# Relu-squared attention and an FFN on one core: when the casting transfers start, when beta is made, and where the first FFN1 matmuls stand

## The chip, the cores and the metric

The kernel runs on one core of a Trainium2 chip. A core has four compute engines that run their own instruction streams: TensorE (PE, matmuls), VectorE (DVE), ScalarE (ACT) and GpSimd (POOL). SyncE (SP) issues transfers; ACT and POOL can issue transfers as well. All transfers of the core are carried by its 16 DMA engines. Transfers issued by POOL may change the type on the way (here float32 in memory to bfloat16 on the core); those issued by SP and ACT copy as they are. The metric is the device time of the whole program in microseconds (us); lower is better.

## The reference

Inputs are q, k, v of shape (8, 12, 448, 64), two weight matrices and a vector alpha, all float32.

```python
scores = scale * np.matmul(q, k.transpose(0, 1, 3, 2))     # scale = 1/8
attn = np.maximum(scores, 0.0) ** 2 / S                    # S = 448
x = np.matmul(attn, v)                                     # (8, 12, 448, 64)
x = x.transpose(0, 2, 1, 3).reshape(3584, 768)
h = x @ w_in                                               # 768 -> 2048
g = np.maximum(h, 0.0) + alpha * np.minimum(h, 0.0)        # alpha: one value for each of 2048
out = g @ w_out                                            # 2048 -> 768, float32
```

There is no softmax: a score is clipped at zero and squared. Each (batch, head) pair is independent in the attention; the FFN mixes the 12 heads of a batch.

## The kernel before, in words

**Quads.** Four heads of one batch make a quad; a batch has three, so there are 24 quads, numbered 0 to 23. The 448 positions of a head are 64 times 7. A score block `j` (0 to 6) of a quad holds 64 key positions of each of the four heads against all 448 queries: four matmuls of 64x64 weights and 448 columns, into two halves of PSUM (`score_mm`, L158).

**One quad's work.** `load` (float32, from SP) or `load_bf16` (casting, from POOL, L102) brings k, q and v. `transpose` (L133, L108) turns k and q on PE for quads 0 to 5 and copies the result out of PSUM into `kT` and `qT`; later quads are turned by transfers. `scores` runs one block and clips it at zero on ACT, on DVE, or half on each ("both"); `squares2` squares two blocks at once on DVE (L202). `attnv` (L233) multiplies the seven squared blocks with v, and its result is scaled into `xT` (L242 to L248).

**The FFN.** `ffn1(b, ff, kms)` (L262) makes 128 of the 2048 columns of one batch in six steps `km` of 128 rows, two steps for each quad of the batch: km 0 and 1 need quad 0, km 2 and 3 quad 1, km 4 and 5 quad 2. ACT then makes `neg` (L269) and DVE combines it with `beta = 1 - alpha` (L270). `ffn2` (L278) does the second matrix for two batches together.

**Order.** The schedule is written by hand: each engine runs its instructions in the order in which the program emits them, and waits at an instruction until what it needs is there. Buffers come from pools that rotate: the tile asked for next takes the oldest buffer, and its first writer waits for the last reader of what was in it. Pools that matter here: `mm_ps` (four PSUM banks, tags "mm"), `sc_ps` (two), and `early_pool` (two buffers for each of k and q in bfloat16, so that quad 2's k takes the buffer of quad 0's).

**The start.** `warm(18)` (L367) runs 18 matmuls on zeros. SP loads quad 0's raw q, then its raw k in two parts (blocks 0 to 2, then 3 to 6), then alpha (L373 to L378). POOL makes two identity matrices and issues the casting loads of quad 1's k and q and of v for quads 0 and 1 (L381 to L384). DVE and ACT cast quad 0's q and k (L386 to L392), PE turns them. The loop at L398 then goes through the blocks of quads 0 to 2, with the transposes of the next quad at blocks 3 and 4, and `attnv` of the quad before at block 2. After quad 0's blocks, alpha (16 by 128) is turned on PE into a column for each of 128 rows (L422), DVE makes beta (L423), and POOL's next loads are emitted: quad 2, w_in in three pieces, quad 3. In the last quad of the loop, blocks 4, 5 and 6 are each followed by the first four km of one `ffn1` of batch 0 (L419).

**After the start.** Batch 0's remaining FFN1 and the blocks of quads 3, 4 and 5 are interleaved by a list (L458 to L466), in which `turn(n)` transposes quad n. The rest of the program, from L477, spreads score blocks of later batches between FFN matmuls.

Of the kernel before, what the change touches and what calls it, by code (L numbers as in the profile page):

```python
# [10 lines left out]
F32 = mybir.dt.float32  # L11
BF16 = mybir.dt.bfloat16
ACTF = mybir.ActivationFunctionType
ALU = mybir.AluOpType
# [6 lines left out]
NJ = 7  # L21
# [3 lines left out]
def kernel(  # L25
# [10 lines left out]
    nc = tc.nc  # L36
    B, H, S, D = q.shape
# [5 lines left out]
    KF = d_ff // 128  # L43
# [4 lines left out]
    def pool(name, bufs, **kw):  # L48
        return ctx.enter_context(tc.tile_pool(name=name, bufs=bufs, **kw))
# [6 lines left out]
    early_pool = pool("early", 2)  # L56
# [10 lines left out]
    mm_ps = pool("mmps", 4, **PSUM)  # L67
# [3 lines left out]
    alpha_sb = singles.tile([KF, 128], F32)  # L71
    beta_sb = singles.tile([128, KF], F32)
    ident_f = singles.tile([KF, KF], F32)
# [5 lines left out]
    raw, cast, qT, kT, vb = {}, {}, {}, {}, {}  # L79
    src = {"q": q, "k": k, "v": v}  # L80

    def flat(n, w):
        b, g = quads[n]
        return src[w][b, 4 * g:4 * g + 4].rearrange("(s hf) (pp j) d -> (hf pp) s (j d)", hf=2, j=NJ)
# [10 lines left out]
    def load_bf16(n, names="kqv"):  # L95

        for w in names:
            if w == "v":
                t = vb[n] = v_pool.tile([128, 2, NJ, D], BF16, tag="v", name="vb")
            else:  # L100
                t = cast[(n, w)] = early_pool.tile([128, 2, NJ, D], BF16, tag=w, name=f"{w}e")
            nc.gpsimd.dma_start(out=t.rearrange("p s j d -> p s (j d)"), in_=flat(n, w))  # L102

    def copy(eng, o, i):
        if eng is nc.scalar:
            nc.scalar.copy(o, i)
        else:
            eng.tensor_copy(o, i)  # L108
# [12 lines left out]
    def transpose(n, w, js=range(NJ), eng=None):  # L121
        store = qT if w == "q" else kT
        if n not in store:
            store[n] = qkT_pool.tile([128, NJ, 2, PP], BF16, tag=w, name=f"{w}T")
        t, dst = cast[(n, w)], store[n]
        if n >= n_pe:
            nc.sync.dma_start_transpose(out=dst.rearrange("p j h c -> p j (h c)"),
                                        in_=t.rearrange("p j s d -> p (j s d)"))
            return
        ps = mm_ps.tile([128, NJ, 2 * PP], BF16, tag="mm", name="tps")  # L130
        for j in js:
            for s in range(2):
                nc.tensor.transpose(ps[64 * s:64 * s + 64, j], t[:, s, j], ident)  # L133
        lo, hi = js[0], js[-1] + 1
        copy(eng or nc.vector, dst[:, lo:hi].rearrange("p j h c -> p j (h c)"), ps[:, lo:hi])
# [4 lines left out]
    def load_w_in(lo, hi):  # L140
        for hf in range(2):
            for e in range(2):
                nc.gpsimd.dma_start(out=w_in_sb[64 * hf:64 * hf + 64, :, e, lo:hi],
                                    in_=w_in_v[hf, e, :, :, lo:hi])
# [37 lines left out]
    def scores(n, j, relu="act", space=sc_ps, pair=False):  # L182

        ps, half = score_tile(space)
        score_mm(n, j, half)
        rl = relu_tile(pair)
        if relu in ("both", "act2"):
            relu_half(rl, half, 0, nc.scalar)
            relu_half(rl, half, 1, nc.vector if relu == "both" else nc.scalar)
        elif relu == "dve":  # L190
            nc.vector.tensor_scalar(rl, ps[:, :, :S], 0.0, None, ALU.max)
        else:
            nc.scalar.activation(rl, ps[:, :, :S], ACTF.Relu)  # L193
        todo.append((n, j, rl))

    def squares2(keep=0):

        while len(todo) >= 2 + keep:
            two = [todo.pop(0) for _ in range(2)]
            t = pairs.pop(0)  # L200
            a = at2_pool.tile([128, 2, 2, S], BF16, tag="at2", name="atp")
            nc.vector.tensor_tensor(a, t, t, ALU.mult)  # L202
            for i, (n, j, _) in enumerate(two):
                att[(n, j)] = a[:, i]
# [50 lines left out]
    def ffn1(b, ff, kms=range(KM)):  # L255
        if b % 2 == 0 and ff == 0 and kms[0] == 0:
            gT[b // 2] = g_pool.tile([128, KF, 2 * S], BF16, tag="g", name="gT")
        if kms[0] == 0:
            hps[ff] = mm_ps.tile([128, S], F32, tag="mm", name="hps")
        ps = hps[ff]  # L260
        for km in kms:
            nc.tensor.matmul(ps, w_in_sb[:, km // 2, km % 2, bass.ts(ff, 128)],  # L262
                             xT[b][:, km // 2, km % 2, :],
                             start=(km == 0), stop=(km == KM - 1))
        if kms[-1] != KM - 1:
            return

        neg = neg_pool.tile([128, S], F32, tag="neg", name="neg")
        nc.scalar.activation(neg, ps, ACTF.Relu, scale=-1.0)  # L269
        nc.vector.scalar_tensor_tensor(gT[b // 2][:, ff, (b % 2) * S:(b % 2) * S + S],  # L270
                                       neg, beta_sb[:, ff:ff + 1], ps, ALU.mult, ALU.add)
# [91 lines left out]
    def warm(count):  # L363

        ps = sc_ps.tile([128, 2, 512], F32, tag="sc", name="warm")
        for _ in range(count):
            nc.tensor.matmul(ps[:, 0, :256], warm_w, warm_x, start=True, stop=True)  # L367

    for w in "qk":
        raw[(0, w)] = raw_pool.tile([128, 2, NJ, D], F32, tag=w, name=f"{w}raw")  # L370
        cast[(0, w)] = early_pool.tile([128, 2, NJ, D], BF16, tag=w, name=f"{w}e")
    first, rest = range(0, 3), range(3, NJ)
    nc.sync.dma_start(out=raw[(0, "q")].rearrange("p s j d -> p s (j d)"), in_=flat(0, "q"))  # L373
    for js in (first, rest):
        lo, hi = js[0], js[-1] + 1
        nc.sync.dma_start(out=raw[(0, "k")][:, :, lo:hi].rearrange("p s j d -> p s (j d)"),
                          in_=flat(0, "k")[:, :, lo * D:hi * D])
    nc.sync.dma_start(out=alpha_sb, in_=moe_alpha.rearrange("(kf p) -> kf p", p=128))  # L378
    make_identity(nc, ident)
    make_identity(nc, ident_f)  # L380
    load_bf16(1, "k")  # L381
    load_bf16(1, "q")
    load_bf16(0, "v")
    load_bf16(1, "v")  # L384
    warm(18)
    nc.vector.tensor_copy(cast[(0, "q")][:, 0], raw[(0, "q")][:, 0])  # L386
    nc.scalar.copy(cast[(0, "q")][:, 1], raw[(0, "q")][:, 1])
    transpose(0, "q")
# [5 lines left out]
    scores(0, 1, pair=True)  # L394
    scores(0, 2, "both", mm_ps, pair=True)
    transpose(0, "k", rest)
    squares2(keep=1)
    for n in range(NG):  # L398
        last = n == NG - 1
        for j in range(NJ):  # L400
            if n == 0 and j < 3:
                continue
            if last and j == 6:
                scores(n, j)
                squares2()
            elif j == 5 and not last or j == 2:
                scores(n, j, "both", mm_ps, pair=True)
            else:
                scores(n, j, "dve" if last and j == 4 else "act", pair=True)
            if not (last and j == 6):  # L410
                squares2(keep=1)
            if j == 2 and n > 0:
                attnv(n - 1, space=mm_ps)
            if j == 3 and not last:
                transpose(n + 1, "k")
            if j == 4 and not last:
                transpose(n + 1, "q")
            if last and j >= 4:
                ffn1(0, j - 4, range(0, 4))  # L419
        if n == 0:  # L420
            ps = mm_ps.tile([128, KF], F32, tag="mm", name="aps")
            nc.tensor.transpose(ps, alpha_sb, ident_f)  # L422
            nc.vector.tensor_scalar(beta_sb, ps, -1.0, 1.0, ALU.mult, ALU.add)  # L423
            load_bf16(2)
            load_w_in(0, 512)
            load_w_in(512, 1024)
            load_w_in(1024, 2048)
            load_bf16(3)
# [4 lines left out]
    attnv(2, range(0, 4), apart=True)  # L433
    attnv(2, range(4, NJ))
    ffn1(0, 3, range(0, 4))
    def turn(n):
        return lambda: (transpose(n, "k", eng=nc.scalar), transpose(n, "q"))

# [16 lines left out]
    for ff in range(4):  # L455
        ffn1(0, ff, range(4, KM))
    f = [fn for _, fn in steps(0, "in")]
    play([f[4], f[5], f[6], turn(3), f[7], f[8], g("30", "31", "32"), f[9], f[10], f[11], f[12],  # L458
          g("33", "34", "35"), f[13], f[14], f[15]])
    load_bf16(5)  # L460
    load(6, after=w_out_sb[:, 0, 384:385])
    load(7)
    o = [lambda c=c, hf=hf, h=h: ffn2(0, c, hf, h) for hf in range(2) for c in range(3) for h in range(2)]
    play([g("36"), turn(4), o[0], o[1], g("40", "41", "3a"), o[2], o[3], g("42", "43", "44"), o[4], o[5],
          g("45", "46"), o[6], turn(5), o[7], g("50", "51", "4a"), feed(6, "k", "q"), o[8], o[9],
          g("52", "53", "54"), feed(6, "v"), o[10], g("55", "56"), feed(7, "k", "q"), o[11]])  # L466

# [64 lines left out]
```

## Time and profile before

| what | value |
|---|---|
| median of 6 runs | 398.9 us (397.05 to 400.43) |
| the profiled execution | 398.75 us, of which its span 397.0 |
| PE busy | 385.8 us |
| DVE, ACT, POOL busy | 261.0, 220.4, 72.5 us |
| casting queue (q0) | 9.96 MB written on the core, 15.9% of the 16 DMA engines' time over the span |
| plain loads and stores from SP (q1) | 44.78 MB, 43.9% |
| raw q of quad 0, issued / its casts begin | 0.74 / 4.08 us |
| second part of raw k, its cast begins | 8.17 us |
| alpha, issue to landing | 6.1 us, issued at 2.26 |

The span runs from the first to the last instruction of the profiled execution, and times in the text are counted from its start. The page cuts the span into 40 equal slices and gives each engine's busy share of a slice in tenths. "The chain that ended last" is followed back from the last instruction, at each step to what released it. A row of a timeline gives start, length, engine, line, operation, written tile <- read tiles, and in brackets how long the engine had stood idle before it and what ended that. For transfers, q0 are the casting ones that POOL issues, q1 those of SP, q10 those of ACT.

### The profile page before, as it was taken

How to read it: one execution, taken by the hardware profiler on the slowest of the kernel's cores; microseconds unless marked ns; L12 is line 12 of the kernel's file. 1: busy time of each engine (PE TensorE's matmuls, PEld its weight loads, DVE VectorE, ACT ScalarE, POOL GpSimd, SP SyncE). 2: the span in 40 equal slices, each digit the busy share in tenths (PEclk: the TensorE clock that was granted, in tenths of full speed). 3: DMA queues.
4: the chain of work that ended last, by engine and by line, in shares of the span. 5: the costliest groups of instructions: out<-in, count | busy, mean ns of one | idle time of the engine just before them, and what ended most of it. 6: DMA issues, size and time to landing. Idle time of an engine off the chain costs nothing.

```text
span 397.0 us, 7955 instructions
## 1 busy us (share of the span) xinstructions
PE 385.8 (97%) x3213; PEld 201.7 (51%) x3213; DVE 261.0 (66%) x406; ACT 220.4 (56%) x345; POOL 72.5 (18%) x87
## 2 busy tenths in 40 slices
PE   7898999999999999999999999999999999999996
PEld 4444555445555455544555445554555545555564
DVE  3976955677675877577665897768575676636421
ACT  5875856675555674466553765556455475624200
POOL 4764000022032430032020550032002300000000
PEclk9899999999999999999999999999999999999999
DMA  8999998593579923492097951295048820120033
GB/s 173 145 207 206 203 216 275 129 302 43 150 139 218 291 84 88 110 294 47 2 216 216 263 163 30 68 265 175 2 132 179 223 46 2 41 74 7 0 81 79
DMA packets 64756, 55.44 MB, mean 140 GB/s; under 512 B 35776, under 2 KB 60496, under 8 KB 64720
## 3 DMA queue, kind: packets, MB, share of 16 engines
q1 hardware_dynamic: 53504, 44.78, 43.9%
q0 software_dynamic: 10976, 9.96, 15.9%
q8 instruction: 25, 0.41, 0.4%
q10 hardware_dynamic: 240, 0.20, 0.2%
q14 instruction: 11, 0.09, 0.1%
HBM read 45.62 MB, written 11.01 MB: 143 GB/s over the span
## 4 chain that ended last, share of the span: by engine, by line
PE 86%; DVE 5%; DMA 4%; ACT 2%; issue 1%; SPq 0%; ACTq 0%; DVEq 0%
PE ops L278 36%; PE hps L262 32%; PE av L233 7%; PE sc L158 5%; PE sch L158 4%; DMA qe<-in_q_dram 3%; DVE at L213 2%; DMA kraw<-in_k_dram 2%; PE ops L301 1%; PE tps L133 1%; DVE atp L202 1%; ACT rl L193 1%; DVE rlp L167 1%; ACT rl L165 1%; DVE gT L270 0%
## 5 line engine op out<-in xcount | busy, mean ns | idle before, releaser
L262 PE MATMUL hps<-xT,w_in_sb 128*128 128x448 bf16 x768 | 151.1, 353 | 1.6 <-DVE gT L270 1.0
L278 PE MATMUL ops<-w_out_sb,gT 128*128 128x384 bf16 x864 | 147.9, 327 | 0.0
L278 PEld LDWEIGHTS <-gT 128*128 128x128 bf16 x864 | 81.1, 98 | 64.9 <-issue 14.2
L213 DVE TENSOR_TENSOR at<-rl 128x896 bf16<-128x896 bf16 x147 | 102.9, 721 | 16.8 <-ACT rl L193 7.0
L262 PEld LDWEIGHTS <-w_in_sb 128*128 128x128 bf16 x768 | 73.2, 98 | 76.1 <-issue 11.1
L270 DVE SCALAR_TENSOR_TENSOR gT<-neg,beta_sb,hps 128x448 bf16<-128x448 f32 x128 | 83.7, 676 | 34.9 <-ACT neg L269 34.8
L269 ACT ACTIVATE neg<-hps 128x448 f32<-128x448 f32 x128 | 68.4, 553 | 59.0 <-PE hps L262 54.9
L193 ACT ACTIVATE rl<-sc 128x896 bf16<-128x896 f32 x95 | 83.3, 926 | 1.5 <-PE sc L158 1.5
L165 ACT ACTIVATE rl<-sch 128x448 bf16<-128x448 f32 x67 | 34.8, 543 | 76.2 <-PE sch L158 76.2
L286 DVE COPY osb<-ops 128x384 f32<-128x384 f32 x54 | 29.9, 555 | 51.6 <-PE ops L278 51.5
L108 POOL CAST kb<-kraw 128x896 bf16<-128x896 f32 x16 | 14.9, 934 | 208.6 <-DMA kraw<-in_k_dram 201.0
L158 PE MATMUL sc<-qT,kT 64*64 64x448 bf16 x440 | 33.9, 356 | 2.7 <-ACT rlp L193 1.8
L167 DVE TENSOR_SCALAR rl<-sch 128x448 bf16<-128x448 f32 x39 | 24.2, 621 | 15.4 <-PE sch L158 15.4
L233 PE MATMUL av<-at,vb 64*64 64x448 bf16 x592 | 32.0, 349 | 0.0
L158 PEld LDWEIGHTS <-kT 64*64 64x64 bf16 x672 | 14.6, 106 | 27.9 <-issue 23.4
L233 PEld LDWEIGHTS <-vb 64*64 64x64 bf16 x672 | 19.9, 107 | 13.0 <-issue 1.4
L248 ACT ACTIVATE xT<-av 128x896 bf16<-128x896 f32 x21 | 19.4, 922 | 7.4 <-PE av L233 7.3
L158 PE MATMUL sch<-qT,kT 64*64 64x448 bf16 x232 | 22.4, 375 | 0.0
L108 POOL CAST qb<-qraw 128x896 bf16<-128x896 f32 x16 | 18.5, 1159 | 0.0
L108 POOL CAST vb<-vraw 128x896 bf16<-128x896 f32 x16 | 18.5, 1159 | 0.0
L193 ACT ACTIVATE rlp<-sc 128x896 bf16<-128x896 f32 x14 | 12.2, 933 | 2.2 <-PE sc L158 2.2
L202 DVE TENSOR_TENSOR atp<-rlp 128x1792 bf16<-128x1792 bf16 x10 | 10.8, 1087 | 0.4
(54 smaller groups left out, 89.1 us busy)
## 6 DMA issues: line engine op xcount, KB each, us to landing
out_dram<-osb SPq DMA_DIRECT2D x54, 192.0 KB, 2.8
qraw<-in_q_dram SPq DMA_DIRECT2D x19, 448.0 KB, 4.8
kraw<-in_k_dram SPq DMA_DIRECT2D x18, 448.0 KB, 5.3
vraw<-in_v_dram SPq DMA_DIRECT2D x18, 448.0 KB, 5.9
w_out_sb<-in_moe_w_out_dram POOLq DMA_DIRECT2D x2, 1536.0 KB, 20.2
w_in_sb<-in_moe_w_in_dram POOLq DMA_DIRECT2D x8, 192.0 KB, 8.5
w_in_sb<-in_moe_w_in_dram POOLq DMA_DIRECT2D x4, 384.0 KB, 9.9
vb<-in_v_dram POOLq DMA_DIRECT2D x6, 224.0 KB, 9.8
```

The source lines that it names most:

```text
L108: eng.tensor_copy(o, i)
L158: nc.tensor.matmul(half[r][64 * c:64 * c + 64, :S], kT[n][64 * r:64 * r + 64, j, c, :], qT[n][64 * r:64 * r + 64, :, c, :], start=True, st ...
L165: nc.scalar.activation(rl[:, r], half[r][:, :S], ACTF.Relu)
L167: nc.vector.tensor_scalar(rl[:, r], half[r][:, :S], 0.0, None, ALU.max)
L193: nc.scalar.activation(rl, ps[:, :, :S], ACTF.Relu)
L213: nc.vector.tensor_tensor(a, rl, rl, ALU.mult)
L233: nc.tensor.matmul(half[r][64 * s:64 * s + 64, :S], vb[n][64 * r:64 * r + 64, s, j, :], a[64 * r:64 * r + 64, s], start=(j == 0), stop=(j ...
L262: nc.tensor.matmul(ps, w_in_sb[:, km // 2, km % 2, bass.ts(ff, 128)], xT[b][:, km // 2, km % 2, :], start=(km == 0), stop=(km == KM - 1))
L269: nc.scalar.activation(neg, ps, ACTF.Relu, scale=-1.0)
L270: nc.vector.scalar_tensor_tensor(gT[b // 2][:, ff, (b % 2) * S:(b % 2) * S + S], neg, beta_sb[:, ff:ff + 1], ps, ALU.mult, ALU.add)
L278: nc.tensor.matmul(ps, gT[sb][:, ff, bass.ts(c, 128)], w_out_sb[:, ff, bass.ts(hf, 384)], start=(ff == 0), stop=(ff == KF - 1))
L286: nc.vector.tensor_copy(o[:, bass.ts(hf, 384)], ps)
```

## The change

Alpha's load moves from the end of SP's four loads to ACT, ahead of everything else that ACT does. POOL copies one column of alpha into the buffer of quad 1's k before it issues the load of that buffer, so that this load, and all that POOL issues after it, comes after alpha's landing; the same transfers follow in the same order. The first run of zero matmuls has 15 in place of 18. Alpha's transpose and beta move from the end of quad 0's blocks to right after the second transposes of quad 0's k. In quad 2, the four steps of `ffn1(0, 0)` after block 4 become three after block 4 and one after block 5; `ffn1(0, 1)` still follows block 5 and `ffn1(0, 2)` block 6.

```diff
+    nc.scalar.dma_start(out=alpha_sb, in_=moe_alpha.rearrange("(kf p) -> kf p", p=128))
     for w in "qk":
         raw[(0, w)] = raw_pool.tile([128, 2, NJ, D], F32, tag=w, name=f"{w}raw")
...
-    nc.sync.dma_start(out=alpha_sb, in_=moe_alpha.rearrange("(kf p) -> kf p", p=128))
     make_identity(nc, ident)
     make_identity(nc, ident_f)
-    load_bf16(1, "k")
+
+    cast[(1, "k")] = early_pool.tile([128, 2, NJ, D], BF16, tag="k", name="ke")
+    nc.gpsimd.tensor_copy(cast[(1, "k")][:KF, 0, 0, 0:1], alpha_sb[:, 0:1])
+    nc.gpsimd.dma_start(out=cast[(1, "k")].rearrange("p s j d -> p s (j d)"), in_=flat(1, "k"))
     load_bf16(1, "q")
     load_bf16(0, "v")
     load_bf16(1, "v")
-    warm(18)
+    warm(15)
...
     transpose(0, "k", rest)
+    ps = mm_ps.tile([128, KF], F32, tag="mm", name="aps")
+    nc.tensor.transpose(ps, alpha_sb, ident_f)
+    nc.vector.tensor_scalar(beta_sb, ps, -1.0, 1.0, ALU.mult, ALU.add)
     squares2(keep=1)
...
-            if last and j >= 4:
-                ffn1(0, j - 4, range(0, 4))
+
+            if last and j == 4:
+                ffn1(0, 0, range(0, 3))
+            if last and j == 5:
+                ffn1(0, 0, range(3, 4))
+                ffn1(0, 1, range(0, 4))
+            if last and j == 6:
+                ffn1(0, 2, range(0, 4))
         if n == 0:
-            ps = mm_ps.tile([128, KF], F32, tag="mm", name="aps")
-            nc.tensor.transpose(ps, alpha_sb, ident_f)
-            nc.vector.tensor_scalar(beta_sb, ps, -1.0, 1.0, ALU.mult, ALU.add)
             load_bf16(2)
```

## The prediction

> **What bounds the kernel now.** I read the page first (busy time, then the 40 slices), then the chain that ended last, then the order of work around the places it names.
>
> ```profile
> span 397.0 us, 7955 instructions
> PE 385.8 (97%) x3213; PEld 201.7 (51%) x3213; DVE 261.0 (66%) x406; ACT 220.4 (56%) x345; POOL 72.5 (18%) x87
> PE   7898999999999999999999999999999999999996
> DMA  8999998593579923492097951295048820120033
> ```
>
> TensorE (PE) is busy for 97%, and its only weak slices are among the first four and the last: a slice is 9.9 us, so what an edit can win lies ahead of about 40 us. Busy times by stretch say the same: in 36.46 to 390 us PE is busy for 352.32 of 353.54. The work in that stretch stays in its order, so the change is worth what it moves the point 36.46. The chain around that point, and PE just ahead of it:
>
> ```profile
> 24.71 11.12 DMA qe<-in_q_dram
> 35.83 0.04 issue
> 35.88 0.58 PE tps L133 x14
> 36.46 2.38 PE hps L262 x12
> ```
> ```profile
> 34.77 0.58 PE L133 MATMUL tps<-ident,ke 128*64 128x128 bf16 x14 [0.51 <-DMA ke<-in_k_dram]
> 35.88 0.58 PE L133 MATMUL tps<-ident,qe 128*64 128x128 bf16 x14 [0.52 <-DMA qe<-in_q_dram]
> ```
>
> These are quad 3's casted k and q. PE had nothing to do for 0.51 and 0.52 us: **the queue of casting transfers, not PE, sets 36.46**. PE's own lead over the queue is 0.51 us at k and 1.03 us at q. That queue is one line of transfers in order of issue (quads 1 and 2, w_in, quad 3, ...), so quad 3 lands when everything ahead of it has gone through. How full it was, by stretch (all queues' bytes):
>
> ```profile
> DMA packets 604, 0.51 MB, mean 169 GB/s; under 512 B 49, under 2 KB 604, under 8 KB 604
> q0 software_dynamic: 436, 0.37, 85.0%
> q1 hardware_dynamic: 168, 0.14, 21.5%
> ```
> ```profile
> DMA packets 299, 0.27 MB, mean 106 GB/s; under 512 B 20, under 2 KB 298, under 8 KB 298
> ...
> DMA packets 418, 0.36 MB, mean 121 GB/s; under 512 B 28, under 2 KB 418, under 8 KB 418
> ...
> DMA packets 2594, 3.23 MB, mean 202 GB/s; under 512 B 194, under 2 KB 1827, under 8 KB 2593
> ```
>
> The first fence is 4.75 to 7.75 us: casting (q0) and the plain loads of quad 0 (q1) share the engines. The second has 9.75 to 12.25 us (106 GB/s), 14 to 17 (121) and 17 to 33 (202: full). In 7.75 to 9.75 q0 moved 461 packets, 230 per us. So there are two thin stretches. The first has a cause in the chain of the front and in POOL's order:
>
> ```profile
> 1.75 6.40 DMA kraw<-in_k_dram
> 8.14 0.02 issue
> 8.17 0.43 DVE ke L392
> 8.60 0.53 DVE rlp L167
> 9.13 0.42 DVE kT L108
> ```
> ```profile
> 9.61 0.72 POOL L102 DMA_DIRECT2D ke<-in_k_dram  x1 [4.99 <-DVE kT L108]
> ```
>
> The second part of quad 0's raw k lands only at 8.14, because the casts of quad 1 crowd it out; its kT copy ends at 9.53, and only then may POOL issue quad 2's k (9.61: it reuses quad 0's buffer). By then the four casts of quad 1 are nearly through, and the queue runs thin.
>
> **The change, part by part.**
>
> *Casts behind alpha.* ACT issues alpha at about 0.75, ahead of its table load (0.75 to 2.03, now some 0.45 later, the length of SP's q issue; ACT then sat idle for 2.04 until raw q at 4.08, so it is covered). When does alpha land? Row: alpha issued on SP at 2.26 took 6.1 us, behind all of raw q and k; so taken from ACT, 6.9. Rule: the Trainium skill, "DMA: Bandwidth & Descriptors", section "Queues, rings and completion order", says that each DMA engine goes round the queue rows packet by packet, so 16 small packets on ACT's row don't wait for SP's. The trace shows it only for two other queues, which moved 436 and 168 packets side by side (above). Nearest row for that: raw q, issued at 0.74, had its first packets at 1.9, and its casts began 0.45 after its last packet. That gives 2.4 at the earliest, 4.08 (raw q itself) at the latest for the rule; I take 3.0. By the row the casts would start at 7.1 and the sum below would be 3.9 us worse, some 402; by the rule it is what follows. I take the rule, since the 6.1 is the place behind SP's loads. POOL's one-column copy costs 0.18 (the row of the same copy at L91), so quad 1's k is issued at 3.2 in place of 1.63. Behind it on POOL wait 3 more casts and then quad 2's, nothing else. First packets came 3.17 after the first issue (4.80), 1.0 after that of 9.61 (10.62). I take 3.17, the row of the queue's first use: 6.4. With 1.0 it would be 4.2, before the raw k is through.
>
> *Raw k alone.* Raw q and k are 896 KB; 1.5 to 4.5 us moved 0.74 MB of it, so without casts the rest is through by about 4.7 and landed by 5.2 instead of 8.14.
>
> *Shorter warm-up.* 18 matmuls on zeros ran for 4.00 us, to 5.13; 15 take 3.33, to 4.46. The q casts end at 4.64, and the transposes began at 5.06: they now begin at 4.70, 0.36 earlier, after a gap of 0.24.
>
> *The front after that.* qT copy 5.70 to 6.32; raw k's second cast on DVE 6.32 to 6.75 (was 8.17); first kT 6.5, scores from 6.55 (was 6.91); relu half 7.3 to 7.95; second kT copy to 8.37 (was 9.53). The alpha transpose (0.28 on PE) lies under that copy, and beta (0.17 on DVE) under the wait for ACT's second relu (to 8.7): both cost nothing, and beta's 0.17 leaves DVE's full stretch at 14.69. If ACT were early, 0.17 would show. Its buffer shifts the ring of four: quad 1's k transposes now wait for ACT's half relu of block 2, to 9.3, where PE would be at 8.8. So: k transposes 9.3 (was 9.90), q 10.3 (was 11.30), fifth score block 10.9 (was 12.19). From there DVE and ACT are full, as before; DVE's third square is done 0.9 earlier, and with beta gone the front stands 1.0 to 1.1 earlier. Quad 1's k must be there at 9.3: 6.4 + 1.4 to 1.9 (272 packets at 200 to 145 per us) + 0.7 from last packet to PE (as at 34.03 and 34.77) = 8.5 to 9.0. Just in time.
>
> *The clock.*
>
> ```profile
> 6.50:9.90 3.40, 1.76 (x26) 0.63 (x25) 1.92 (x5) 2.52 (x4) 0.29 (x1) 1.00 1.22 193
> 9.90:13.30 3.40, 3.40 (x49) 1.94 (x45) 3.04 (x5) 2.32 (x4) 3.40 (x6) 0.51 0.92 130
> ```
>
> Columns: length, then PE, PEld, DVE, ACT, POOL busy, granted clock, DMA share, GB/s. After 1.76 busy of 3.40 the next 3.40 ran at 0.51: 14 transposes took 0.95 there, 0.58 at 16.65. The Trainium skill, "TensorE: Matmul & The Clock Gate", section "HAM oscillation — how this bites in real kernels", asks for no idle gap over about 3.4 us. The longest here was 0.98, so by the rule the clock should have held and closing gaps wins nothing; by the row a half-busy window lost it. By the row the changed window has scores and transposes earlier (some 2.7 busy of 3.4) and the clock may hold, which the times of "the front" need in part: without it they are 0.4 later on each set of 14 transposes. Either way this is PE's lead, which is not what sets 36.46. It also speaks against cutting the warm-up: a 0.24 gap in the window before. I cost it at nothing, at 1.2 us of lead if the clock came a window later.
>
> *FFN1 behind the scores.* PE waited 0.33 at 23.74 for the copy of xT (L244). Now three of the first four matmuls go ahead, and the fourth after the next scores: up to 0.33 of lead, less where the next score's buffer waits for the DVE relu ending at 24.68. I take 0.2. Same matmuls, none added.
>
> *Sum.* PE's lead grows by 1.1 + 0.2 = 1.3. It counts only with the queue. The queue's side: by 12.25 it had moved 436 + 461 + 298 = 1195 packets. Starting at 6.4 and never thin (quad 2's k is issued at 8.4), it moves (12.25 - 6.4) x 230 = 1345, less 87 to 255 for a slow start (3 us at 201 or 145 per us, the rates of all queues and of q0 in 4.75 to 7.75, in place of 230): 1090 to 1258, so 0.3 earlier to 0.5 later. In 14 to 17 the missing (202 - 121) x 3 = 0.24 MB are 1.2 us; no view tells why. Were it late issues, then with POOL's issues 1.2 earlier it fills; else nothing. Bounds: 0.5 later to 1.5 earlier; I take 0.6 earlier, near the middle. PE's lead (1.3 + 0.51) covers it. So 36.46 becomes 35.9, PE's waits at quad 3 grow from 1.0 to about 1.7, and the end moves by 0.6. The profiled execution took 398.75 (span 397.0, 1.75 around it): 398.15. The median, 398.9, is 0.15 above it: **398.3**.
>
> Later transfers don't bind: quad 4 landed some 2 us ahead of its transposes at 48.62, and w_out's second half at about 56 ahead of its use at 62.
>
> **Rivals.**
>
> *The queue fills both thin stretches, or alpha is at 2.4* (396.8). For: the issue of quad 2 is 1.2 earlier. Then up to 1.5 + 0.6 earlier; PE's 1.3 + 1.03 allows 2.3 at most: 396.6 at the best. Executions of before reach down to 397.05. Against: in 14 to 17 the issues were already 4 us ahead of their packets.
>
> *Alpha lands late* (slower, 400.0). Place: POOL's copy, with every cast behind it, and PE's alpha transpose ahead of the fourth scores. If alpha lands with the raw k at 5.0, the casts are issued at 5.2, first packets at 8.4, quad 1's k usable at 10.3 to 11, over 1 us after PE wants it; the queue stands 1.4 later than before at its worst, 1.1 in the middle. It decides from a landing at 3.6 on (0.6 to lose); each us more costs one. Past 0.5% from 5.6.
>
> *It doesn't do what it says* (398.9 to 399.4). Raw k may have been slow for its 1 KB rows, not for the casts; then kT's copy stays at 9.5 and the queue starts late for nothing. Against: its packets thinned from 59 to 10 per quarter us just as the casts began.
>
> **How the numbers follow.** The measurement can tell about 0.5%, 2.0 us: faster is below 396.9, slower above 400.9. Forecast (queue 0 to 1.3 earlier, 397.6 to 398.9): 0.50. Queue filled: 0.22. Alpha late: 0.15, a third of it past the bound. No effect: 0.13. Two in ten left out at both ends: 396.6 to 400.3. Faster 0.19 (most of the second case), slower 0.09 (a late alpha, or a clock that comes late as well), same 0.72.
>
> **What would show it.** Alpha landing near 3.0; raw k landed near 5.2 and its second cast near 6.3; POOL's quad 2 issue near 8.4; no thin stretch at 9.75 to 12.25; the clock near 1.0 in 9.9 to 13.3; and PE's two waits at quad 3 grown to about 1.7 together. It is wrong if those waits shrink, if alpha lands past 4, or if the time moves by something behind 40 us.

## The result and the profile after

The changed kernel takes 397.22 us (median of 35 runs, 396.01 to 400.32) against 398.05 of the kernel before (median of 72 runs, 396.08 to 401.43). The ratio is 0.9977 with a 95% interval of 0.9965 to 0.9989: 0.8 us faster by the medians. The interval ends below 1, and the step is smaller than the 0.5% that the forecast took for the least that can be told. The forecast was 0.6 us, from 398.9 (the median of six runs) to 398.3; the larger set puts the kernel before at 398.05.

The page of the profiled execution (398.36 us, of which its span 396.5), with its PE and DMA rows by slice:

```profile
span 396.5 us, 7951 instructions
PE 384.6 (97%) x3210; PEld 201.6 (51%) x3210; DVE 258.8 (65%) x406; ACT 220.3 (56%) x345; POOL 72.9 (18%) x88
...
PE   7698999999999999999999999999999999999996
...
DMA  8999997592579923492098951295058820120033
```

By this page alone nothing has happened at the front. The front's own rows say otherwise. POOL's order, and the cast of the second part of raw k on DVE:

```profile
3.21 0.18 POOL L383 CAST ke<-alpha_sb 16x1 bf16<-16x1 f32 x1 [1.60 <-DMA alpha_sb<-in_moe_alpha_dram]
3.70 0.84 POOL L384 DMA_DIRECT2D ke<-in_k_dram  x1 [0.31 <-POOL ke L383]
...
6.28 0.67 DVE L395 CAST ke<-kraw 128x512 bf16<-128x512 f32 x1
...
8.09 0.72 POOL L102 DMA_DIRECT2D ke<-in_k_dram  x1 [1.39 <-DVE rlp L167]
```

Alpha is there at 3.2, raw k's second cast starts at 6.28 in place of 8.17, and quad 2's k is issued at 8.09 in place of 9.61. The casting queue in the two stretches that were thin, 9.75 to 12.25 and 14 to 17 us:

```profile
DMA packets 498, 0.42 MB, mean 167 GB/s; under 512 B 31, under 2 KB 498, under 8 KB 498
...
DMA packets 631, 0.57 MB, mean 191 GB/s; under 512 B 45, under 2 KB 631, under 8 KB 631
```

They held 299 and 418 packets before, at 106 and 121 GB/s; both are fuller. And yet the chain at quad 3, and PE's waits there:

```profile
25.16 10.75 DMA qe<-in_q_dram
35.91 0.04 issue
35.95 0.58 PE tps L133 x14
36.53 2.38 PE hps L262 x12
```
```profile
34.82 0.58 PE L133 MATMUL tps<-ident,ke 128*64 128x128 bf16 x14 [0.61 <-DMA ke<-in_k_dram]
35.95 0.58 PE L133 MATMUL tps<-ident,qe 128*64 128x128 bf16 x14 [0.55 <-DMA qe<-in_q_dram]
```

Quad 3's transposes end at 36.53; before it was 36.46. In this execution the whole front came to nothing at the point that counts, and the 0.4 us by which its span is shorter (396.5 against 397.0) lie elsewhere. Two things had to be found out: why a fuller queue landed no earlier, and whether the gain in the median is the queue's at all.

### The profile page after: what moved, and what is told of

Its sections match the earlier page's. It is cut to its first block, busy times and chain, and to the rows that moved or that the text cites. A ratio compares the mean times of both kernels' runs of the same rounds, so it can differ in the third digit from the quotient of the medians.

```text
span 396.5 us, 7951 instructions
## 1 busy us (share of the span) xinstructions
PE 384.6 (97%) x3210; PEld 201.6 (51%) x3210; DVE 258.8 (65%) x406; ACT 220.3 (56%) x345; POOL 72.9 (18%) x88
## 4 chain that ended last, share of the span: by engine, by line
PE 87%; DMA 8%; DVE 2%; ACT 1%; issue 1%; ACTq 0%; POOLq 0%
PE ops L278 36%; PE hps L262 33%; PE av L233 7%; PE sc L158 4%; PE sch L158 4%; DMA qe<-in_q_dram 3%; DMA w_in_sb<-in_moe_w_in_dram 2%; DVE at L213 2%; DMA ke<-in_k_dram 2%; PE ops L301 1%; DMA qraw<-in_q_dram 1%; PE tps L133 1%; ACT rl L193 0%; ACT rl L165 0%; DVE gT L270 0%
## 5 line engine op out<-in xcount | busy, mean ns | idle before, releaser
L262 PEld LDWEIGHTS <-w_in_sb 128*128 128x128 bf16 x768 | 73.2, 98 | 75.7 <-issue 10.3
L213 DVE TENSOR_TENSOR at<-rl 128x896 bf16<-128x896 bf16 x147 | 100.2, 701 | 17.6 <-ACT rl L193 7.5
L270 DVE SCALAR_TENSOR_TENSOR gT<-neg,beta_sb,hps 128x448 bf16<-128x448 f32 x128 | 83.9, 676 | 36.2 <-ACT neg L269 36.0
L165 ACT ACTIVATE rl<-sch 128x448 bf16<-128x448 f32 x67 | 34.8, 543 | 76.2 <-PE sch L158 76.2
L233 PEld LDWEIGHTS <-vb 64*64 64x64 bf16 x672 | 20.7, 110 | 14.1 <-issue 1.9
```

What stands on the lines that cost most here:

```text
L165: nc.scalar.activation(rl[:, r], half[r][:, :S], ACTF.Relu)
L213: nc.vector.tensor_tensor(a, rl, rl, ALU.mult)
L233: nc.tensor.matmul(half[r][64 * s:64 * s + 64, :S], vb[n][64 * r:64 * r + 64, s, j, :], a[64 * r:64 * r + 64, s], start=(j == 0), stop=(j ...
```

## A second profile of both kernels

**Both kernels once more.** One execution is one throw, so a second one of each was profiled.

> The kernel before again, for a second look at where quad 3's transposes end (36.46 us in the first), when the second part of raw k is cast (8.17), where the clock is low, and how long everything behind quad 3 takes (360.5). If the raw k is late because the casts crowd it, its time should vary with the first cast packet (4.7 in the first look).

> The changed kernel again, for a second look. Its first profile had one of the 16 DMA engines 1.1 us behind the other 15 at quad 3, and its transposes there ended at 36.53 us. If that engine is chance, they end near 35.0 to 35.5 in this look; if it belongs to the change, at 36.5 again.

Quad 3's transposes in the second profile of before, then in that of the changed kernel:

```profile
34.10 0.58 PE L133 MATMUL tps<-ident,ke 128*64 128x128 bf16 x14 [0.86 <-DMA ke<-in_k_dram]
35.19 0.58 PE L133 MATMUL tps<-ident,qe 128*64 128x128 bf16 x14 [0.51 <-DMA qe<-in_q_dram]
```
```profile
33.69 0.58 PE L133 MATMUL tps<-ident,ke 128*64 128x128 bf16 x14 [1.20 <-DMA ke<-in_k_dram]
34.82 0.58 PE L133 MATMUL tps<-ident,qe 128*64 128x128 bf16 x14 [0.55 <-DMA qe<-in_q_dram]
```

They end at 35.77 and 35.40. PE's waits are 1.37 and 1.75; the forecast for the changed kernel was 1.7. In all four profiles PE waits for the transfer.

A transfer has landed when all 16 DMA engines have reported. The trace has each report; these are those of quad 3's k, in us:

```
                8th engine   15th    16th (landed)
before             33.47    34.66    34.73
before, again      32.59    33.70    34.06
after              31.83    33.64    34.78
after, again       31.94    33.34    33.64
```

In the mean of two profiles the eighth engine is through 1.1 us earlier (33.03 to 31.89), the last one 0.2 (34.40 to 34.21): in the first profile of the changed kernel the last is 1.1 behind the fifteenth. It was as far behind at v of quad 0 (11.67 against 10.59), but not all the way between: at one piece of w_in the two reported at 22.13 and 22.20. What counts is the slowest of the 16, and packets counted over all of them don't show it. Which engine it is, the trace doesn't name.

Two profiles of each are few. Ten of this study's fourteen have quad 3's loads in the same place, with alpha in time or not waited for. The six with the casts at once landed quad 3's k between 33.97 and 35.78, 34.8 in the mean; the four with the casts behind the early alpha between 33.13 and 34.78, 33.8 in the mean. That is 1.0 us earlier, 0.6 without the two of the six in which the clock was half for three windows (below); the eighth engine is 1.4 earlier (33.5 to 32.1). So over more executions the landing does come earlier, by a little less than the mean engine.

What lies behind quad 3 (span less the end of its transposes) is 360.5 in both profiles of before and 360.0 in both of the changed kernel. Over the 14 profiles of this study, all with the same matmuls behind that point, it goes from 359.0 to 360.5 with no order by kernel (the casts alone 359.4, the last experiment below 360.3). PE's waits for `gT` (DVE, L270) go with it: short ones of 0.2 to 0.6 us at 137 to 317 us, none in the two profiles with 359.0, four in one of 360.5. So it is scatter, and a single pair of spans can't tell 0.5 us here.

**The clock of every execution.** Part of the gain goes through TensorE's clock. Each execution has its mean granted clock on record, profiled or not. In the profiles of this study the clock falls to half for one, two or three windows of 3.41 us among the first 23 us, and the means are then 0.994 to 0.996 (one), 0.991 (two) and 0.987 (three); without such a fall they are 0.999 or more. By this, for the 119 executions of before that were measured beside the experiments and the 36 listed for the changed kernel (executions, median time in us):

| mean granted clock | before | changed kernel |
|---|---|---|
| 0.998 and above: no half window | 43, 397.56 | 24, 397.19 |
| 0.994 to 0.996: about one | 55, 398.36 | 12, 397.90 |
| 0.991 and below: two or more | 21, 398.70 | 0 |

A half window is rarer in the changed kernel, and executions with one are slower by 0.7 to 0.8 us in both. At an equal clock the changed kernel is ahead by 0.4 to 0.5. If each row of before is weighted as in the changed kernel, some 0.3 us of the gain is the rarer half clock and the rest the difference at equal clock; this is an estimate, since the two sets were not measured at the same time. The experiment with 18 zero matmuls below was measured beside before and agrees: 19 of its 22 executions have no half window, against 19 of 43, and those are 0.5 us apart (396.73 against 397.25).

## The change taken apart

**The casts behind alpha, alone.**

```diff
+    nc.scalar.dma_start(out=alpha_sb, in_=moe_alpha.rearrange("(kf p) -> kf p", p=128))
     for w in "qk":
...
-    nc.sync.dma_start(out=alpha_sb, in_=moe_alpha.rearrange("(kf p) -> kf p", p=128))
...
-    load_bf16(1, "k")
+    cast[(1, "k")] = early_pool.tile([128, 2, NJ, D], BF16, tag="k", name="ke")
+    nc.gpsimd.tensor_copy(cast[(1, "k")][:KF, 0, 0, 0:1], alpha_sb[:, 0:1])
+    nc.gpsimd.dma_start(out=cast[(1, "k")].rearrange("p s j d -> p s (j d)"), in_=flat(1, "k"))
```

> The kernel before with one part of the change: alpha is issued on ACT and the casts of quad 1 follow its landing; warm-up, beta and FFN1 stay as they were. Theory Q (the casting queue and its slowest DMA engine set the transposes of quad 3): the queue is the same as in the changed kernel, so most of the gain is here, ratio to before 0.998 to 0.999. Theory F (PE's front sets it, the changed kernel gains through all its parts): a share of the gain, and the waits at quad 3 stay at about 1.0 us. Theory N (the change does nothing at the front, the 0.2% are scatter): 1.000.

Measured: 0.9970 (0.9950 to 0.9989). This part alone has a gain as large as the whole change's; the interval holds the changed kernel's 0.9977. Raw k's second cast starts at 6.50, quad 2's issue is at 8.31, and in this profile no engine lags at quad 3 (15th at 33.12, 16th at 33.13):

```profile
33.17 0.58 PE L133 MATMUL tps<-ident,ke 128*64 128x128 bf16 x14 [0.18 <-DVE gT L270]
34.30 0.58 PE L133 MATMUL tps<-ident,qe 128*64 128x128 bf16 x14 [0.55 <-DVE gT L270]
```

The view names DVE, but q landed at 34.26 and its transposes began at 34.30: both semaphores are waited for, and DVE's came last by the profile. Against the first profile of before the queue is 1.6 earlier, and so is the end of quad 3's transposes (34.88); against the second, both are 0.9 earlier. The queue side of the theory stands, and PE had the lead for it with the old warm-up, beta and FFN1.

**All but the waiting casts.**

```diff
-    nc.gpsimd.tensor_copy(cast[(1, "k")][:KF, 0, 0, 0:1], alpha_sb[:, 0:1])
```

> The changed kernel without POOL's copy, so the casts of quad 1 start at once as in the kernel before; alpha still on ACT, short warm-up, early beta, FFN1 moved. Theory Q: the raw k lands near 8.1 us again, the queue is that of before and the time that of before, 0.9995 to 1.001. Theory F: beta, warm-up and FFN1 bring part of the gain, 0.998 to 0.999. Theory N: as the changed kernel.

Measured: 1.0029 (1.0008 to 1.0051), slower than before. That is above all three ranges, though the interval reaches down to the upper end of theory Q's. The raw k's second cast starts at 9.16, quad 2's issue is at 10.83, and these are the stretches of the clock (length, then PE, PEld, DVE, ACT, POOL busy, granted clock, DMA share, GB/s), followed by quad 3:

```profile
5.90:9.31 3.41, 1.32 (x21) 0.45 (x16) 0.78 (x2) 2.64 (x4) 0.00 (x0) 1.00 1.17 207
9.31:12.72 3.41, 2.77 (x31) 1.56 (x31) 2.72 (x6) 0.92 (x1) 1.89 (x3) 0.50 0.69 89
12.72:16.13 3.41, 2.89 (x38) 1.42 (x38) 3.31 (x5) 2.81 (x4) 3.40 (x7) 0.50 1.13 164
16.13:19.55 3.42, 3.42 (x42) 1.70 (x35) 2.79 (x4) 1.82 (x4) 1.77 (x3) 0.50 1.12 158
```
```profile
36.84 0.58 PE L133 MATMUL tps<-ident,ke 128*64 128x128 bf16 x14
37.26 0.56 PE L133 MATMUL tps<-ident,qe 128*64 128x128 bf16 x14
```

No wait at quad 3: the transfers are late too (k landed at 35.78), but PE is later still, after 10 us at half clock. So PE's front can be the bound, when the clock falls for three windows. By the granted clocks that is so in 4 of this kernel's 11 executions, with a median of 399.6, against 3 of 41 of before beside it; its other seven have 398.4, near before's 398.3. To find which of the three remaining parts costs it, each was put into the kernel before alone.

> The kernel before with 15 zero matmuls in place of 18 and nothing else. By the prediction's sum: 0.36 us of PE's lead, none of the queue's, so no difference, 0.9985 to 1.0015. If the shorter warm-up is what made the changed kernel without the waiting casts slower (1.0029), by a window of low clock more, this is slower, 1.002 to 1.004.

> The kernel before with alpha on ACT and beta made early, without the copy that makes the casts wait. The raw k stays late (8 us), so PE's alpha transpose and DVE's beta stand at a place where both are wanted, and the ring of four buffers is shifted. By the prediction's sum nothing, 0.9985 to 1.0015; if this is what made the changed kernel without the waiting casts slower, 1.002 to 1.004.

> The kernel before with the first FFN1 matmuls placed as in the changed kernel and nothing else. PE's wait of 0.33 us for the copy of xT should go, which is lead that the queue then takes back: no difference, 0.9985 to 1.0005. If PE's front sets quad 3 in most executions, 0.9990 to 0.9995, which these rounds can hardly tell from nothing.

```diff
-    warm(18)
+    warm(15)
```
```diff
+    nc.scalar.dma_start(out=alpha_sb, in_=moe_alpha.rearrange("(kf p) -> kf p", p=128))
...
-    nc.sync.dma_start(out=alpha_sb, in_=moe_alpha.rearrange("(kf p) -> kf p", p=128))
...
     transpose(0, "k", rest)
+    ps = mm_ps.tile([128, KF], F32, tag="mm", name="aps")
...
         if n == 0:
-            ps = mm_ps.tile([128, KF], F32, tag="mm", name="aps")
```
```diff
-            if last and j >= 4:
-                ffn1(0, j - 4, range(0, 4))
+            if last and j == 4:
+                ffn1(0, 0, range(0, 3))
+            if last and j == 5:
+                ffn1(0, 0, range(3, 4))
+                ffn1(0, 1, range(0, 4))
+            if last and j == 6:
+                ffn1(0, 2, range(0, 4))
```

The warm-up, beta and FFN1 measured, in this order: 1.0009 (0.9988 to 1.0031), 1.0006 (0.9987 to 1.0026), 1.0001 (0.9984 to 1.0017). None can be told from nothing; the intervals reach from some 0.6 us faster to 1.2 slower. The short warm-up's profile has the same fall of the clock, half from 8.5 to 18.7 us, and its quad 3 ends at 37.49. By the granted clocks all 14 of its executions had a half window and 4 of them three, with beta 8 and 4 of 14, with FFN1 12 and 3 of 14; of before beside them 25 and 2 of 35. So the fall of three windows is commoner with each of the three parts, and only with the short warm-up does every execution have a half window; which of them makes the 1.0029 stays open. In the profile of FFN1 alone the 0.33 wait for xT's copy is gone, as the diff says, and quad 3 ends at 36.48.

**The warm-up, in the changed kernel.**

```diff
-    warm(15)
+    warm(18)
```

> The changed kernel with 18 zero matmuls at the start in place of 15. By the sum of the prediction the transposes begin some 0.2 us later, all of it PE's lead and none of it the queue's: the time of the changed kernel, ratio 0.9965 to 0.999. If the shorter warm-up costs by a colder clock, this is faster than the changed kernel by up to 1 us.

Measured: 0.9972 (0.9957 to 0.9988), the changed kernel's time. The two first rows of transposes, with 15 and with 18:

```profile
4.79 0.91 PE L133 MATMUL tps<-ident,qe 128*64 128x128 bf16 x14 [0.30 <-DVE qe L389]
```
```profile
5.06 0.78 PE L133 MATMUL tps<-ident,qe 128*64 128x128 bf16 x14
```

They do start 0.27 earlier with 15, after a gap of 0.30, and no gain from it can be seen. At quad 3 this profile has k's transposes at 34.30, 0.65 after k's landing and without a wait, and q's at 34.77, 0.04 after q's landing at 34.73: PE and the queue arrive together, and the queue still comes last.

**Alpha late.**

```diff
-    nc.scalar.dma_start(out=alpha_sb, in_=moe_alpha.rearrange("(kf p) -> kf p", p=128))
...
+    nc.sync.dma_start(out=alpha_sb, in_=moe_alpha.rearrange("(kf p) -> kf p", p=128))
     make_identity(nc, ident)
```

> The changed kernel with alpha issued last on SP, behind raw q and raw k, and the casts still behind alpha: the rival of a late alpha, made on purpose. Alpha should land near 6 us in place of 3.15, the first cast packet near 8 in place of 5.3. Theory Q: the whole queue is 2 to 2.7 us later than in the changed kernel, PE waits longer at quad 3, ratio to before 1.001 to 1.005. Theory F (the queue does not bind): only quad 1's transposes wait, some 1 us at the front, ratio 0.998 to 1.0.

Measured: 1.0031 (1.0016 to 1.0046), 1.2 us slower than before and about 2 slower than the changed kernel, for this:

```profile
5.99 0.18 POOL L383 CAST ke<-alpha_sb 16x1 bf16<-16x1 f32 x1 [4.38 <-DMA alpha_sb<-in_moe_alpha_dram]
6.48 0.84 POOL L384 DMA_DIRECT2D ke<-in_k_dram  x1 [0.31 <-POOL ke L383]
```
```profile
10.71 0.58 PE L133 MATMUL tps<-ident,ke 128*64 128x128 bf16 x14 [2.24 <-DMA ke<-in_k_dram]
...
36.33 0.58 PE L133 MATMUL tps<-ident,ke 128*64 128x128 bf16 x14
37.00 0.58 PE L133 MATMUL tps<-ident,qe 128*64 128x128 bf16 x14
```

Alpha comes 2.8 later, the first cast packet too (8.04 against 5.26), and PE stands 2.24 for quad 1's k. At quad 3, k had landed at 35.81 and its transposes ran at 36.33, held up by PE's own front, with the clock half from 12.2 to 19.0; q landed at 36.95 and its transposes began 0.05 later, so the queue set the end here by a little. A half clock belongs to this kernel: 20 of its 22 executions have two or more half windows, against 8 of 43 of before beside it, and the profile's fall follows a window in which PE stood waiting for quad 1's k and was busy for 0.90 of 3.41. The rival's mechanism is real, at quad 1 as much as at quad 3; its price was set too high. By the forecast's scale (nothing left of the gain at a landing of 3.6, one us for each us more) a landing at 5.94 costs 2.3; the 1.1 of the forecast was for one at 5.0, and 1.2 was measured.

## The queue taken out of the way

If quad 3's landing is what stands in the way, its k and q can go ahead of w_in's third piece, which is needed only after them.

```diff
-            load_w_in(1024, 2048)
-            load_bf16(3)
+            load_bf16(3, "kq")
+            load_w_in(1024, 2048)
+            load_bf16(3, "v")
```

> The kernel before with the same reordering of quad 3's k and q. Theory Q: its two waits (0.51 and 0.52 us) go, 1.0 us, ratio 0.997 to 0.998, and the difference to c_after is what the change brings to PE's front once the queue no longer binds, 0.5 to 1.3 us. Theory F: no difference to before, and c_after ahead of it by the 0.8 us that the changed kernel is ahead.

> The changed kernel with the casting loads of quad 3's k and q issued ahead of w_in's third piece, so that they are landed some 7 us earlier and can't hold PE; w_in's third piece then lands near 36, about when it is wanted. Theory Q: PE's two waits at quad 3 (0.61 and 0.55 us in its profile) go and all of PE's lead shows, 1.1 to 1.6 us below the changed kernel, ratio to before 0.994 to 0.9955. Theory F: those waits cost nothing that the front does not set, ratio near 0.997.

Measured: 0.9965 (0.9950 to 0.9980) on the kernel before and 0.9956 (0.9937 to 0.9975) on the changed one. Quad 3's transposes in the latter:

```profile
32.48 0.58 PE L133 MATMUL tps<-ident,ke 128*64 128x128 bf16 x14
32.89 0.56 PE L133 MATMUL tps<-ident,qe 128*64 128x128 bf16 x14
```

No wait, and they end at 33.45, 2 to 3 us earlier than in the two profiles of the changed kernel (34.77 on the kernel before). On the kernel before, moving two loads is worth 1.4 us by the ratio, against 0.9 for the change; the two intervals overlap. It isn't the clock: in executions without a half window it is 396.08 (9 of 22) against 397.61 for before beside it (14 of 41), 1.5 apart. So the waits at quad 3 were the bound of the kernel before. In the changed kernel they are in both profiles, and the step from 0.9977 to 0.9956 points the same way, but the intervals overlap. That the difference between the two is the lead that the change brings to PE's front (0.4 us by the ratios, 1.3 by the two profiles) is inside the intervals and not shown.

Last, the same reordering with only the casts behind alpha, and the old warm-up, beta and FFN1.

> The kernel before with two edits: the casts behind alpha, and quad 3's k and q ahead of w_in's third piece; warm-up, beta and FFN1 as before. With the queue out of the way PE's lead shows: if those three parts bring the 0.36 + 0.17 + 0.2 us that the prediction gave them, this is some 0.5 us above the kernel with the whole change and the same reordering (0.9956), so 0.9965 to 0.9975; if they bring nothing, 0.9950 to 0.9962.

Measured: 0.9934 (0.9910 to 0.9957, on 6 runs), 395.83 us. Its quad 3 ends at 33.81. It lies with the 0.9956 of the kernel that has all parts, the intervals overlapping, and its own interval ends below the 0.9965 that was to be had at least if the other three parts brought their 0.7 us (a bound that takes the 0.9956 as exact). In executions without a half window the two have 395.82 (all 6) and 395.85 (10 of 13). So where the lead could show, these three brought nothing that was measured. By their medians both versions lie below the kernel before and the changed kernel.

## Why the prediction was right, and where its steps were not

- **The bound.** Quad 3's landing, not PE's front, was said to set the time. The reordered loads show it (0.9965), and so do the four profiles of the two kernels, all with PE waiting there. It isn't so in every execution: where the clock was half for three windows (all but the waiting casts, the short warm-up alone) PE came later than both transfers.
- **Alpha.** Taken at 3.0 by the rule of the Trainium skill's page "DMA: Bandwidth & Descriptors", section "Queues, rings and completion order", against a row that said 6.9. Alpha landed at 3.15 and POOL's copy began at 3.21. The trace agrees with the rule: alpha's 32 packets on q10 (16 had been counted) began between 1.83 and 2.84 us, among those of raw q on q1, which began at 1.86 and landed at 4.28. The row's 6.1 us was not the place behind SP's loads alone: with no cast in flight (the late alpha) the same place took 3.7, from 2.27 to 5.94, so some 2.4 of it were the casts. The rule decided the sign of the forecast.
- **The start of the casts.** Two sizes were off. POOL's issue came at 3.70 in place of 3.2, since it waits 0.31 for POOL's own copy. The first packet came 1.56 after the issue, not 3.17 (in before it was in fact at 4.74, 3.1 after). Together 5.26 in place of 6.4, a term missed by 1.1 us. Why it is 2.2 to 3.1 where the issue stands at 1.63 isn't shown; the plain loads in flight are not the whole of it, since it is 1.56 both beside raw k's last packets (the changed kernel) and with all of them landed (the late alpha).
- **Raw k.** Landed at 5.61, forecast 5.2; cast at 6.28, forecast 6.32; quad 2's issue at 8.09, forecast 8.4. The rival that raw k is slow by its rows falls: in the profiles without the wait the first cast packet was at 3.8 to 4.7 and the cast at 7.5 to 9.2; with the wait on the early alpha (4.9 to 5.4) the cast was at 6.0 to 6.5.
- **The queue's sum.** It said 0.6 earlier, between 0.5 later and 1.5 earlier, and over ten profiles the landing is 0.6 to 1.0 earlier. Two of its terms were wrong and pull against each other. With the first packet at 5.26 its own working gives 0.7 to 1.4 earlier for the first thin stretch alone, in place of 0.5 later to 0.3 earlier. And packets counted over 16 engines are right for the mean engine at most, while the slowest sets the landing: the last stood 1.3 us behind the eighth with the casts at once, 1.7 behind the early alpha (means of the six and the four profiles). That the 0.6 came near is partly luck.
- **PE's lead.** Waits of 1.16 and 1.75 at quad 3, 1.7 forecast. That warm-up, beta and FFN1 are worth nothing while the queue binds held for each alone, within its interval; the three together without the waiting casts were 1.2 us slower. That they are worth 0.7 us of lead once the queue is out of the way was not borne out.
- **A late alpha.** The sum of this rival doesn't hold to its own terms: first packets at 8.4 make quad 1's k usable at 10.5 to 11.0, not from 10.3, and a start of the queue 2.0 later turns 0.6 earlier into 1.4 later in the middle, which it gives as its worst.
- **Nothing behind 36.46 changes.** True of the program, not of one execution: that part scatters over 1.5 us. The sum against one profiled execution was safe only because the medians were compared in the end.
- **The clock.** It was put down as PE's lead, which was not to count for the time. By the table of granted clocks above some 0.3 us of the gain is the rarer half clock: in an execution with a half window PE's lead can be used up, and then the clock does count. That the clock held through 9.9 to 13.3 in both profiles of the changed kernel proves little by itself, since it held in the second of before too; over the fourteen profiles, four of the seven with the casts at once lost it between 8.5 and 9.9, and none of the six with the casts behind the early alpha before 19.0. In one of the changed kernel's it fell there:

```profile
8.79:12.20 3.41, 2.08 (x48) 1.24 (x47) 3.41 (x5) 3.11 (x5) 3.41 (x7) 1.00 1.19 169
12.20:15.60 3.40, 2.76 (x62) 1.46 (x50) 3.19 (x5) 2.78 (x5) 1.63 (x3) 1.00 1.19 188
15.60:19.03 3.43, 2.12 (x36) 1.11 (x38) 3.41 (x6) 3.43 (x6) 2.00 (x4) 1.00 1.20 182
19.03:22.44 3.41, 3.41 (x40) 2.22 (x36) 2.56 (x4) 1.92 (x4) 1.88 (x3) 0.50 1.23 202
```

A window with PE busy for 2.08 of 3.41 kept the clock, one with 2.12 of 3.43 lost it. Over the fourteen profiles, cut into windows of 3.41 us from their changes of clock on, it was lost after eight windows, with PE busy for 0.90 to 2.12; the least busy one that kept it had 1.66, the next 2.01. The longest idle time of PE in or into the eight was 2.24 us, so the rule of the Trainium skill, "TensorE: Matmul & The Clock Gate", section "HAM oscillation — how this bites in real kernels", to keep idle gaps under about 3.4 us, was not enough here; a busy share near 0.6 looks like the edge, with scatter. Once at half, it came back after windows in which PE was busy throughout (eight times), and stayed at half after five with 2.09 to 3.08.

## What to carry to other kernels

Find the transfer that PE waits for, and first ask whether it can be issued ahead of something that is needed later: two loads moved measured 1.4 us here, against 0.9 for all the work on what stands before them, though the two intervals overlap. Lead that is won on an engine ahead of a bound transfer shows up as a longer wait there, and brought no time that could be measured here. Set times beside the granted clock of each execution: the changed kernel had the half clock less often, and that part of its gain is not the transfer's landing. A transfer in flight beside one that is wanted sooner can be made to wait on a small load that lands at the right time, but it must be a load with nothing in front of it: behind the plain loads, the same wait made the kernel slower than before. The transfers here landed with the slowest of their 16 engines, so a queue's bytes were not enough to say when.

## What had not been expected

- The last of 16 DMA engines can be 1.1 us behind the fifteenth (11.67 against 10.59 at quad 0's v, 34.78 against 33.64 at quad 3's k, together at 22.2 between), in one execution and not in the next of the same kernel (33.64 against 33.34 at quad 3's k).
- The first packet of POOL's casting queue came anywhere from 3.80 to 4.74 us in seven profiles in which its issue stood at the same place of the program (1.62 to 1.63), and from 4.86 to 5.41 in the six where it followed the early alpha. The raw k's time follows it only loosely (9.16 with 3.80, but 7.66 with 4.04).
- The granted clock fell for three windows in a row, 10.2 us, though PE was busy for 2.77 and 2.89 of 3.41 in the first two of them: at half clock only a window without any gap brought it back.
